# Four tiles of the first product by seven products of quarters, and the casts of v on ScalarE

## The chip, the cores and the metric

The kernel runs on one core of one Trainium2 chip, in one launch. The metric is the device time of that launch in microseconds (us). The time before is the median of three runs.

## The reference, cut to what matters

```python
B, H, S, D = 4, 8, 768, 64                      # attention with a decaying state
gamma = 1.0 - 2.0 ** (-5.0 - np.arange(H))
for t in range(S):
    state = gamma * state + outer(k[t], v[t])   # per batch and head, 64 x 64
    y[t] = (1 / sqrt(D)) * q[t] @ state
x = y.transpose(0, 2, 1, 3).reshape(3072, 512)  # tokens x d_model
h = x @ w_in                                    # first product, d_ff = 2048
g = max(h, 0) + alpha * min(h, 0)
out = g @ w_out                                 # second product, 3072 x 512, f32
```

## The kernel before

**Units and blocks.** The tokens are cut into 12 units of 256 (`U`); three units make a batch. Two units make a block of 512 tokens (`TB`), and there are six blocks, 0 to 5 (`NBLK`). The attention of a unit gives its part of `xT`, the transposed input of the first product. All matmuls take f16 and sum in f32 in the eight PSUM banks; the number given to `ps` is the bank, and a new tile in a bank waits until the last reader of the old one is done.

**First product (`ffn1`).** It has 16 tiles of 128 rows of d_ff (`NFT`). A tile is four matmuls, 512 wide, into one bank. Then ScalarE computes `hm = relu(-h)`, and VectorE makes the gate: `gt = hm * (1 - alpha) + h`, in f16. The tile buffers `hm` are three. In blocks 2 to 5 the tiles are made in pairs, 0, 8, 1, 9 and so on to 7, 15 (`HF` is 8).

**Second product (`ffn2_seven`).** In blocks 1 to 5 it is made by seven products of quarters (Strassen's scheme in Winograd's form) instead of eight: the gates are cut in two by d_ff (`k`) and in two by unit, `w_out` likewise. The sums of quarters of `w_out` are made once (`w_sums`, tile `wsum`), those of the gates in each block (`g_sums`, tile `gs`, numbers 0 to 3). Each product is 16 matmuls, 256 wide. The first product reads gate tiles 0 to 7 of the first unit in that order, the second one tiles 8 to 15, the third one `gs` number 1.

**Order.** The scheduling is manual: each engine runs its instructions in the order in which they are issued, and an instruction that waits holds back all behind it on its engine. `ffn1` and `ffn2_seven` are generators, one `yield` for each matmul; `tick(gen, m)` issues m of them. In a block n of the loop at the end, `ffn1(n)` comes first, and between its matmuls GpSimd rescales k and q of the next block's two units (`rescale`, L152) and casts their v (`cast_v`, L168); SP issues the transposes (`turn_dma`) and loads k, q and v of the units after (`load`). Then `ffn2_seven(n)` is issued, and in its gaps the next block's attention: state sums (`sum_mm`, banks 2 and 3), scores (`score_mm`, banks 4 and 5, then 6 and 7), masks on VectorE (`masks`, L280), state updates on VectorE and GpSimd (`state_sum`, L240, L241), and the outputs (`out_mm`), which ScalarE copies to `xT` (`take_y`, L331). VectorE's `g_sums` numbers 0 and 1 are issued after gate tiles (for f below 4 after tile 11, the rest after tile 15), numbers 2 and 3 between the masks. `behind` makes a GpSimd rescale wait for a VectorE sum.

**Copies of results.** In `ffn2_seven`, `kept` copies a bank to an SBUF tile `cu` (ScalarE, L480), and `plus` adds a bank and such a tile into a tile `os` (VectorE, L485), which SP stores.

Of the kernel before, what the change touches and what calls it, by code (L numbers as in the profile page):

```python
# [9 lines left out]
FP = mybir.dt.float32  # L10
F16 = mybir.dt.float16
COPY = mybir.ActivationFunctionType.Copy
SUB = mybir.AluOpType.subtract
RELU = mybir.ActivationFunctionType.Relu
MULT = mybir.AluOpType.mult
# [6 lines left out]
def kernel(  # L22
# [59 lines left out]
    HF, HM = NFT // 2, d_model // 2  # L82
    wsum = sbp.tile([128, 4, HF, HM], F16, tag="wsum", name="wsum")

    def ps(bank, name, dt=FP, n=512):
        return psp.tile([128, n], dt, tag=f"b{bank}", name=name)

# [52 lines left out]
    def unit(u):  # L140
        if u not in prepped:
            prepped[u] = (
                sbp.tile([128, 2, 2, H, D], F16, tag="kdq", bufs=4, name=f"kdq{u}"),
                sbp.tile([128, 4 * NP, 128], F16, tag="kq", bufs=4, name=f"kq{u}"),
                sbp.tile([128, H, 2, D], F16, tag="vx", bufs=4, name=f"vx{u}"),
            )
        return prepped[u]

# [127 lines left out]

    def masks(u, hh, parts=(0, 1)):
        for a in parts:
            m2 = sbp.tile([128, 2, 2, 128], F16, tag=f"m2{a}{hh}", bufs=2, name=f"m2{a}{hh}")
            i = nc.vector.tensor_tensor(  # L280
                out=m2,
                in0=live[u, hh][a].rearrange("p (r a i) -> p r a i", r=2, a=2),
                in1=mask.unsqueeze(2).to_broadcast([128, 2, 2, 128]),
                op=MULT,
            )
            live[u, hh][a] = m2
        return i
# [37 lines left out]
    def take_y(u, cs):  # L325
        n, ul = divmod(u, 2)
        if n not in xT:
            xT[n] = sbp.tile([128, 2, NP, U], F16, tag="xT", bufs=2, name=f"xT{n}")
        ys = live[u]
        for c in cs:  # L330
            nc.scalar.activation(  # L331
                out=xT[n][:, ul, :, 128 * c : 128 * c + 128].rearrange(
                    "k a (p r) -> k a r p", r=2
                ),
                in_=ys[c].rearrange("k (a r p) -> k a r p", r=2, p=64),
                func=COPY,
                bias=0.0,
                scale=1.0,
            )
# [21 lines left out]
        )[i]  # L361
        return nc.vector.tensor_tensor(out=o, in0=a, in1=b, op=op)  # L362

    def ffn1(n, banks, apart=0):


        gt = sbp.tile([128, NFT, TB], F16, tag="gt", bufs=2, name=f"gt{n}")
        gts[n] = gt
        turns = [(f, 2, ul, ul + 1) for ul in range(2) for f in range(0, apart, 2)]
        rest = range(apart, NFT)  # L370
        if apart == 0:
            rest = [f + x for f in range(HF) for x in (0, HF)]
        turns += [(f, 1, 0, 2) for f in rest]
        for i, (f0, nf, lo, hi) in enumerate(turns):
            hps = ps(banks[i % len(banks)], "hps").rearrange("p (f t) -> p f t", f=nf)
            for f in range(nf):
                for hp in range(4):
                    nc.tensor.matmul(  # L378
                        out=hps[:, f, :].rearrange("p (u t) -> p u t", t=U),
                        lhsT=w_in_all[:, hp, 128 * (f0 + f) : 128 * (f0 + f) + 128],  # L380
                        rhs=xT[n][:, lo:hi, hp, :],
                        start=(hp == 0),
                        stop=(hp == 3),
                    )
                    if f < nf - 1 or hp < 3:
                        yield
            hm = sbp.tile([128, TB], FP, tag="hm", bufs=3, name="hm")
            hm = hm.rearrange("p (f t) -> p f t", f=nf)
            nc.scalar.activation(out=hm, in_=hps, func=RELU, bias=0.0, scale=-1.0)  # L389
            for f in range(nf):  # L390
                nc.vector.scalar_tensor_tensor(  # L391
                    out=gt[:, f0 + f, U * lo : U * hi],
                    in0=hm[:, f, :],
                    scalar=oma_sb[:, f0 + f : f0 + f + 1],
                    in1=hps[:, f, :],
                    op0=MULT,
                    op1=ADD,
                )
            if n > 0 and f0 in ((HF + 3, NFT - 1) if apart == 0 else (NFT - 1,)):

                lo = 0 if apart or f0 < NFT - 1 else 4
                hi = HF if f0 == NFT - 1 else 4
                g_sums(n, 0, lo, hi)
                g_sums(n, 1, lo, hi)
            yield

    def ffn2(n, banks, parts=1):
        gt = gts.pop(n)
        opss = {}
        step = NFT // parts  # L410
        for f0 in range(0, NFT, step):
            for tq in range(4):
                if f0 == 0:
                    opss[tq] = ps(banks[tq % len(banks)], "ops")
                for ft in range(f0, f0 + step):
                    nc.tensor.matmul(  # L416
                        out=opss[tq],
                        lhsT=gt[:, ft, 128 * tq : 128 * tq + 128],
                        rhs=w_out_all[:, ft, :],
                        start=(ft == 0),  # L420
                        stop=(ft == NFT - 1),
                    )
                    if ft == NFT - 1:
                        tag = ("os", "cu")[tq % 2]
                        os_sb = sbp.tile([128, d_model], FP, tag=tag, bufs=3, name=tag)
                        nc.scalar.activation(
                            out=os_sb, in_=opss[tq], func=COPY, bias=0.0, scale=1.0
                        )
                        row = TB * n + 128 * tq
                        nc.sync.dma_start(out=out[row : row + 128, :], in_=os_sb)  # L430
                    yield

    def ffn2_seven(n, x, y, z=None):
# [41 lines left out]
                        yield  # L475

        def kept(o):
            t = sbp.tile([128, 2, HM], FP, tag="cu", bufs=3, name="cu")
            for to, i in [(t, o[0])] if o[0] is not None else zip((t[:, 0, :], t[:, 1, :]), o[1]):
                nc.scalar.activation(out=to, in_=i, func=COPY, bias=0.0, scale=1.0)  # L480
            return t

        def plus(o, t, name="os"):
            so = sbp.tile([128, 2, HM], FP, tag=name, bufs=3, name=name)
            nc.vector.tensor_tensor(out=so, in0=o[0], in1=t, op=ADD)  # L485
            return so

# [52 lines left out]
    def tick(gen, m=10**6):  # L540
        for _ in range(m):
            if next(gen, 1) == 1:
                return
# [124 lines left out]
    tick(gen, 9)  # L668
    out_mm(2, (4, 5))
    tick(gen, 10)  # L670
    tick(half, 24)
    turn_pe(3, 0, 6)
    tick(half, 8)
    turn_pe(3, 1, 7)
    tick(gen, 9)
    score_mm(3, 0, (4, 5))
# [26 lines left out]
    for n in range(1, NBLK):  # L703
        more = n + 1 < NBLK
        u0 = 2 * (n + 1)
        if n > 1:
            gen = ffn1(n, (7, 2, 3, 1, 0, 6, 5, 4, 7, 1, 0, 4, 5, 6, 7, 1))
            if more:
                for u in (u0, u0 + 1):
                    i = rescale(G, u, 0, 0, 8)  # L710
                    if u == u0:
                        behind(i, gate)
                    rescale(G, u, 1, 0, 8)
                    turn_dma(u)
                    cast_v(G, u)
                    if u + 2 < NU:
                        load(u + 2)
                    tick(gen, 8)
            tick(gen)
        gen = ffn2_seven(n, 0, 1) if more else ffn2_seven(n, (0, 3), 1, 2)  # L720
        if more:
            tick(gen, 8)
            sum_mm(u0, (2, 3))
            sum_mm(u0 + 1, (2, 3), half=1)
            score_mm(u0, 0, (4, 5))
            score_mm(u0, 1, (6, 7))
            state(u0, 0, G)
            masks(u0, 0)
            s01 = state_sum(u0, 1, G)
            masks(u0, 1, (0,))  # L730
            s10 = state_sum(u0 + 1, 0, G)
            masks(u0, 1, (1,))
            tick(gen, 8)
            state_copy(s01, "aa")
            state_copy(s10)
            tick(gen, 17)
            state(u0 + 1, 1, G)
            g_sums(n, 2, 0, HF)
            tick(gen, 15)
            out_mm(u0, (4, 5))  # L740
            score_mm(u0 + 1, 0, (6, 7))
            score_mm(u0 + 1, 1, (2, 3))
            masks(u0 + 1, 0)
            masks(u0 + 1, 1)
            gate = g_sums(n, 3, 0, HF)
            tick(gen, 32)
            out_mm(u0 + 1, (4, 5))
        else:
            tick(gen, 33)
            g_sums(n, 2, 0, HF)  # L750
            g_sums(n, 3, 0, HF)
        tick(gen)
# [30 lines left out]
```

## Time and profile before

| what | value |
|---|---|
| median of 3 runs | 204.46 us (204.45 to 204.72) |
| the profiled execution | 206.04 us, span 204.3 us |
| instructions in the profile | 5491 |
| TensorE clock granted | full in all 40 slices |
| first product of blocks 2 to 5 (64 matmuls, 512 wide) | 13.8 us each |
| second product with attention, blocks 2 to 4 | 15.9 to 16.0 us each |
| gate (L391), 512 wide | 745 ns mean, x84 |
| relu (L389), 512 wide | 597 ns mean, x96 |
| rescale on GpSimd (L152), 1024 wide | 1902 ns mean, x16 |
| cast of v on GpSimd (L168), 1024 wide | 1037 ns mean, x11 |

In the lines of the profile PE is TensorE's matmuls and PEld its weight loads, DVE is VectorE, ACT is ScalarE, POOL is GpSimd and SP is the queue that issues DMAs. A line of the timeline has the start in us from the span's start, the busy time in us, the engine, the line of the kernel, the operation, output and inputs, shape and number of instructions; in brackets is the idle time before it and what ended it. Shown durations reach from the first element to the end of the write, so consecutive instructions overlap a little: what an instruction costs its engine is the distance from start to start.

### The profile page before, as it was taken

What the parts mean: (1) busy time and instruction counts of PE and PEld (TensorE: products, weight loads), DVE (VectorE), ACT (ScalarE), POOL (GpSimd) and SP (SyncE); (2) the same over time, 40 slices, a digit from 0 to 9 for tenths busy, and PEclk for the clock granted to TensorE, in tenths of its full rate; (3) what the DMA queues carried; (4) which work ended last, traced back from release to release, by engine and by line L of the source; (5) the groups of instructions that cost most, each with busy time, mean ns of one, the idle gap of its engine ahead of it and who ended that gap; (6) DMA issues with size and microseconds to landing.
All of it is one profiled execution on the core that took longest, in us unless ns stands there. A gap on an engine that the chain in (4) does not pass through costs nothing.

```text
span 204.3 us, 5491 instructions
## 1 busy us (share of the span) xinstructions
PE 195.2 (96%) x2314; PEld 128.2 (63%) x2314; DVE 157.0 (77%) x246; ACT 101.9 (50%) x169; POOL 83.3 (41%) x96
## 2 busy tenths in 40 slices
PE   7789997999999999999999999999999999999993
PEld 2457543566574788744788644788544888545882
DVE  7794985646899999189998289996489995589841
ACT  2465665236376333477353466333476254466311
POOL 2289117480269553970065960165930250000000
PEclk9999999999999999999999999999999999999999
DMA  5998999599997799399911499910570011200004
GB/s 158 337 234 134 185 253 235 157 249 173 299 346 223 153 340 304 110 258 304 284 46 41 149 250 281 300 55 22 176 166 0 3 52 57 103 0 0 21 33 154
DMA packets 64696, 33.94 MB, mean 166 GB/s; under 512 B 18064, under 2 KB 64160, under 8 KB 64672
## 3 DMA queue, kind: packets, MB, share of 16 engines
q1 hardware_dynamic: 60272, 29.37, 50.0%
q0 software_dynamic: 4224, 4.19, 13.4%
q8 instruction: 18, 0.29, 0.6%
q10 hardware_dynamic: 176, 0.03, 0.1%
q14 instruction: 6, 0.05, 0.1%
HBM read 27.30 MB, written 6.29 MB: 164 GB/s over the span
## 4 chain that ended last, share of the span: by engine, by line
PE 73%; DMA 16%; DVE 3%; POOL 2%; SPq 2%; issue 2%; ACT 0%; POOLq 0%; DVEq 0%
PE hps L378 32%; PE ox L464 16%; PE oy L464 11%; DMA qs<-in_q_dram 6%; PE ops L416 5%; DMA wout<-in_moe_w_out_dram 4%; DMA win<-in_moe_w_in_dram 4%; DMA ks<-in_k_dram 3%; PE y L313 2%; SPq L132 2%; PE sca L268 2%; PE y L298 1%; POOL tf L241 1%; PE st L215 1%; PE oz L464 1%
## 5 line engine op out<-in xcount | busy, mean ns | idle before, releaser
L378 PE MATMUL hps<-xT,win 128*128 128x512 f16 (+1 forms) x432 | 84.5, 355 | 0.1
L391 DVE SCALAR_TENSOR_TENSOR gt<-hm,oma,hps 128x512 f16<-128x512 f32 (+1 forms) x108 | 70.8, 685 | 13.6 <-ACT hm L389 8.1
L389 ACT ACTIVATE hm<-hps 128x512 f32<-128x512 f32 x96 | 57.3, 597 | 33.6 <-PE hps L378 31.4
L378 PEld LDWEIGHTS <-win 128*128 128x128 f16 x432 | 42.0, 98 | 40.3 <-DMA win<-in_moe_w_in_dram 0.8
L464 PEld LDWEIGHTS <-gs 128*128 128x128 f16 x320 | 31.0, 98 | 3.9
L241 POOL TENSOR_TENSOR tf<-ss,tab 128x256 f32<-128x256 f32 x16 | 12.2, 765 | 35.7 <-DVE ss L240 34.7
L464 PEld LDWEIGHTS <-gt 128*128 128x128 f16 x240 | 22.8, 98 | 4.8
L152 POOL TENSOR_TENSOR kdq<-ks,tab 128x1024 f16<-128x1024 f32 (+1 forms) x10 | 17.3, 1729 | 18.8 <-issue 9.8
L480 ACT ACTIVATE cu<-ox 128x512 f32<-128x512 f32 (+1 forms) x18 | 9.5, 526 | 29.9 <-PE ox L464 29.7
L256 POOL CAST tg<-tf 64x256 f16<-64x256 f32 x29 | 14.2, 488 | 20.0 <-DVE tf L237 18.6
L485 DVE TENSOR_TENSOR os<-oy,cu 128x512 f32<-128x512 f32 x14 | 9.6, 689 | 16.2 <-PE oy L464 13.7
L152 POOL TENSOR_TENSOR kdq<-qs,tab 128x1024 f16<-128x1024 f32 (+1 forms) x13 | 20.7, 1594 | 1.9 <-DMA qs<-in_q_dram 1.9
L280 DVE TENSOR_TENSOR m<-sca,mi 128x512 f16<-128x512 f32 x24 | 16.4, 684 | 4.2 <-PE scb L268 4.2
L464 PE MATMUL ox<-wsum,gs 128*128 128x256 f16 x160 | 19.1, 273 | 0.0
L331 ACT ACTIVATE xT<-y 128x512 f16<-128x512 f32 x24 | 16.2, 741 | 5.6 <-PE y L313 5.5
L280 DVE TENSOR_TENSOR m<-scb,mi 128x512 f16<-128x512 f32 x24 | 16.3, 681 | 0.0
L416 PE MATMUL ops<-wout,gt 128*128 128x512 f16 x64 | 15.2, 380 | 0.2 <-DMA wout<-in_moe_w_out_dram 0.2
L168 POOL CAST vx<-vs 128x1024 f16<-128x1024 f32 (+1 forms) x13 | 12.5, 973 | 5.6 <-DMA vs<-in_v_dram 5.6
L362 DVE TENSOR_TENSOR gs<-gt 128x1024 f16<-128x1024 f16 (+1 forms) x14 | 12.9, 922 | 0.3
L254 ACT ACTIVATE tg<-tf 64x256 f16<-64x256 f32 x11 | 4.6, 414 | 15.6 <-POOL tf L241 10.4
L188 ACT ACTIVATE kq<-trb 128x1024 f16<-128x1024 f16 x8 | 8.2, 1024 | 6.7 <-PE trb L182 6.5
L464 PE MATMUL ox<-wout,gt 128*128 128x256 f16 x80 | 10.4, 274 | 0.0
(50 smaller groups left out, 175.1 us busy)
## 6 DMA issues: line engine op xcount, KB each, us to landing
out_dram<-os SPq DMA_DIRECT2D x21, 256.0 KB, 2.3
vs<-in_v_dram SPq DMA_DIRECT2D x10, 512.0 KB, 6.4
ks<-in_k_dram SPq DMA_DIRECT2D x8, 512.0 KB, 4.6
qs<-in_q_dram SPq DMA_DIRECT2D x8, 512.0 KB, 5.5
ks<-in_k_dram SPq DMA_DIRECT2D x8, 256.0 KB, 4.7
qs<-in_q_dram SPq DMA_DIRECT2D x8, 256.0 KB, 4.8
win<-in_moe_w_in_dram POOLq DMA_DIRECT2D x4, 512.0 KB, 8.0
wout<-in_moe_w_out_dram POOLq DMA_DIRECT2D x4, 512.0 KB, 8.5
```

Source lines behind the costliest of these rows:

```text
L152: return eng.tensor_tensor(out=kdq[:, t, :, h0:h1, :].rearrange("p r h d -> p h r d"), in0=staged[u]["kq"[t]][:, h0:h1, :].rearrange("p h ...
L168: eng.tensor_copy(out=o, in_=i)
L241: eng.tensor_tensor(out=t, in0=ss, in1=dec, op=MULT)
L256: nc.gpsimd.tensor_copy(out=o, in_=i)
L280: i = nc.vector.tensor_tensor(out=m2, in0=live[u, hh][a].rearrange("p (r a i) -> p r a i", r=2, a=2), in1=mask.unsqueeze(2).to_broadcast([ ...
L331: nc.scalar.activation(out=xT[n][:, ul, :, 128 * c : 128 * c + 128].rearrange("k a (p r) -> k a r p", r=2), in_=ys[c].rearrange("k (a r p) ...
L362: return nc.vector.tensor_tensor(out=o, in0=a, in1=b, op=op)
L378: nc.tensor.matmul(out=hps[:, f, :].rearrange("p (u t) -> p u t", t=U), lhsT=w_in_all[:, hp, 128 * (f0 + f) : 128 * (f0 + f) + 128], rhs=x ...
L389: nc.scalar.activation(out=hm, in_=hps, func=RELU, bias=0.0, scale=-1.0)
L391: nc.vector.scalar_tensor_tensor(out=gt[:, f0 + f, U * lo : U * hi], in0=hm[:, f, :], scalar=oma_sb[:, f0 + f : f0 + f + 1], in1=hps[:, f, :],
L416: nc.tensor.matmul(out=opss[tq], lhsT=gt[:, ft, 128 * tq : 128 * tq + 128], rhs=w_out_all[:, ft, :], start=(ft == 0), stop=(ft == NFT - 1),)
L464: nc.tensor.matmul(out=o[1][m], lhsT=lhs(f, m), rhs=rhs(f), start=(first and f == 0 and (m == 0 or o[0] is None)), stop=(f == HF - 1), ski ...
```

## The change

In blocks 2 to 5 `ffn1_mixed` takes the place of `ffn1`. Twelve tiles stay as they were. Tiles 0, 1, 8 and 9 (`SEV` is 2 in each half) are made by seven products of quarters: `w_in` is cut by d_model (`k`) and by d_ff, `xT` by d_model and by unit. Each product p1 to p7 is four matmuls, 256 wide. Bank 4 takes p1, and on top of it p6, p7 and p4; bank 5 takes p2, then p5 and on top of it p3. ScalarE keeps bank 4 after p1, p6 and p7 (`kept`), VectorE adds it to bank 5 after p2, p7 and p3 (`plus`), which gives three of the four result quarters in SBUF. For these, ScalarE makes the relu from SBUF and GpSimd makes the gate by two operations (`gate_pool`: a multiplication and an addition). The fourth, after p4, is gated by VectorE from bank 4 in two halves.

The sums of quarters of `w_in` (`wi_sums`, four operations, 512 wide) are made once, on VectorE between the first gates of block 1. The sums of `xT` (`x_sums`, four operations, 512 wide) are made on VectorE for each of blocks 2 to 5, right after the block's `xT` is complete. The first q rescale of a block on GpSimd waits for them (`xgate`).

The sums of gates (`g_sums` 0 and 1) come in three pieces, for tiles 2 to 4 after tile 12, for 5 to 7 and then 0 and 1 after tile 15. The casts of v for units 8 to 11 move from GpSimd, in the first product, to ScalarE, in the second product of the block before. Buffers: `kdq`, `kq` and `vx` go from 4 to 3, masks and `xT` from 2 to 1, `hm` from 3 to 5, `cu` from 3 to 4.

```diff
-                sbp.tile([128, 2, 2, H, D], F16, tag="kdq", bufs=4, name=f"kdq{u}"),
+                sbp.tile([128, 2, 2, H, D], F16, tag="kdq", bufs=3, name=f"kdq{u}"),
...
+    def x_sums(n):
+        t = sbp.tile([128, 4, 2, U], F16, tag="xsum", name=f"xsum{n}")
+        xsum[n] = t
+        (b11, b21), (b12, b22) = (
+            [xT[n][:, j, 2 * k : 2 * k + 2, :] for k in range(2)] for j in range(2)
+        )
+        t1, t2, t3, t4 = (t[:, y] for y in range(4))
+        for o, a, b in ((t1, b12, b11), (t2, b22, t1), (t3, b22, b12), (t4, b21, t2)):
+            i = nc.vector.tensor_tensor(out=o, in0=a, in1=b, op=SUB)
+        return i
...
+        def relu(i):
+            hm = sbp.tile([128, TB], FP, tag="hm", bufs=5, name="hm")
+            nc.scalar.activation(out=hm, in_=i, func=RELU, bias=0.0, scale=-1.0)
+            return hm
...
+        def gate_pool(i, f, j):
+            hm = relu(i).rearrange("p (f t) -> p f t", f=2)
+            nc.gpsimd.tensor_tensor(
+                out=hm, in0=hm,
+                in1=oma_sb[:, f : f + 2].unsqueeze(2).to_broadcast([128, 2, U]),
+                op=MULT,
+            )
+            nc.gpsimd.tensor_tensor(
+                out=gt[:, f : f + 2, U * j : U * j + U],
+                in0=hm, in1=i.rearrange("p (f t) -> p f t", f=2), op=ADD,
+            )
...
+        order = (
+            "n2:7 n10:2 p1a n3:3 p2a n11:6 g11a p6a n4:1 p5a n12:0 s2:5 p7a n5:7 n13:2 g22a"
+            " p4a n6:3 p3a n14:6 g12a n7:1 n15:7 s5:8 s0:2"
+        )
+        banks = {"a": (4, 5)}
...
-            gen = ffn1(n, (7, 2, 3, 1, 0, 6, 5, 4, 7, 1, 0, 4, 5, 6, 7, 1))
+            gen = ffn1_mixed(n)
...
-                    rescale(G, u, 1, 0, 8)
+                    i = rescale(G, u, 1, 0, 8)
+                    if u == u0:
+                        behind(i, xgate)
                     turn_dma(u)
-                    cast_v(G, u)
+                    if n == 2:
+                        cast_v(G, u)
...
             state_copy(s10)
+            if n > 1 and u0 + 2 < NU:
+                cast_v(A, u0 + 2)
             tick(gen, 17)
...
             out_mm(u0, (4, 5))
+            if n > 1 and u0 + 3 < NU:
+                cast_v(A, u0 + 3)
             score_mm(u0 + 1, 0, (6, 7))
...
             out_mm(u0 + 1, (4, 5))
+            xgate = x_sums(n + 1)
```

In `order`, `n7:1` is tile 7 made whole in bank 1, with its relu and gate; `p6a` is product 6, with the copy or the sum that follows it; `g12a` is the relu and GpSimd's gate of the quarter that the sum after p3 completes (`g11a` after p2, `g22a` after p7); `s2:5` is `g_sums` 0 and 1 for tiles 2 to 4 and 10 to 12.

## The prediction

> **What bounds the kernel now.** I read the page's busy shares first, then the stretches of one steady block, then the timelines of TensorE and VectorE at the seam where the second product begins, because the change reshuffles the first product and the seam is where its results are asked for.
>
> ```profile
> PE 195.2 (96%) x2314; PEld 128.2 (63%) x2314; DVE 157.0 (77%) x246; ACT 101.9 (50%) x169; POOL 83.3 (41%) x96
> ```
>
> ```profile
> core 0: us, PE busy (x) PEld busy (x) DVE busy (x) ACT busy (x) POOL busy (x), PEclk, DMA share, GB/s
> ...
> 114.96:128.77 13.81, 13.81 (x67) 6.25 (x64) 11.93 (x18) 8.96 (x15) 5.80 (x5) 1.00 0.97 252
> 128.77:144.68 15.91, 15.91 (x301) 13.95 (x300) 12.20 (x20) 5.68 (x9) 8.55 (x11) 1.00 0.37 115
> ```
>
> The first stretch is ffn1 of block 3, the second is its ffn2 with the attention of the next block. TensorE is busy in all of both, at full clock: the block has no stall to give back, so a gain can only be TensorE work removed, and any new wait of TensorE is paid in full. VectorE is at 11.93 of 13.81 in ffn1.
>
> ```profile
> 114.96 13.98 PE L378 MATMUL hps<-xT,win 128*128 128x512 f16 x64
> 128.77 1.07 PE L464 MATMUL ox<-wout,gt 128*128 128x256 f16 x8
> ...
> 131.73 1.91 PE L464 MATMUL oy<-wout,gt 128*128 128x256 f16 x16
> 133.48 1.91 PE L464 MATMUL ox<-wsum,gs 128*128 128x256 f16 x16
> ```
>
> ```profile
> 124.81 5.54 DVE L391 SCALAR_TENSOR_TENSOR gt<-hm,oma,hps 128x512 f16<-128x512 f32 x8
> 130.38 0.69 DVE L362 TENSOR_TENSOR gs<-gt 128x1024 f16<-128x1024 f16 x1
> 131.11 0.69 DVE L362 TENSOR_TENSOR gs<-gs,gt 128x1024 f16<-128x1024 f16 x1
> 131.72 0.41 DVE L240 TENSOR_TENSOR ss<-tf,st 128x256 f32<-128x256 f32 x1
> ```
>
> ```profile
> 128.10 2.25 DVE L391 SCALAR_TENSOR_TENSOR gt<-hm,oma,hps 128x512 f16<-128x512 f32 x3
> ```
>
> One 512-wide matmul is 13.81 / 64 = 0.2158 us from start to start, a 256-wide one 1.75 / 16 = 0.1094. Gates (L391) follow each other at (128.10 - 124.81) / 5 = 0.658 and take 0.745. The last three gates start at 128.10, 128.76 and 129.60. Tile 7 is the last but one, so its gate ends at 129.50. The first product of ffn2 reads tiles 0 to 7 in order and wants tile 7 at 128.77 + 7 x 0.1094 = 129.54. The slack is 0.04 us: whatever makes the gate of tile 7 later stops TensorE.
>
> **The change, part by part.** *TensorE.* Four tiles of four 512-wide matmuls (16 x 0.2158 = 3.45) become seven products of four 256-wide ones (28 x 0.1094 = 3.06): 0.39 us less in each of four blocks, 1.56 in all. That price holds for weights that change at every matmul, as in the rows of L464.
>
> *VectorE in ffn1.* Out go four gates (4 x 0.658 = 2.63). In come three sums of PSUM and SBUF (like L485, 0.60 from start to start: 134.78 to 135.38), two half gates (by-form rows give 745 ns for 512 wide and 476 for 256, so 0.658 - 0.27 = 0.39 each), and the sums of gates in three pieces instead of two. Total 2.58 plus about 0.3: VectorE gets 0.25 more work in a stage that is 0.39 shorter. How long a piece of sums takes: 2048 wide 1.14, 1024 wide 0.61, so 768 is about 0.475 and 512 0.345, plus 0.12 for one that needs the one before (131.11 - 130.38 = 0.73).
>
> *The queue, from the stage's first matmul as zero.* A tile takes 0.863 on TensorE and a quarter product 0.4375, so the order ends tiles and products at: 2 at 0.86, 10 at 1.73, p1 2.16, 3 at 3.03, p2 3.46, 11 at 4.33, p6 4.77, 4 at 5.63, p5 6.07, 12 at 6.93, p7 7.37, 5 at 8.23, 13 at 9.09, p4 9.53, 6 at 10.39, p3 10.83, 14 at 11.69, 7 at 12.56, 15 at 13.42. ScalarE's relu starts 0.20 after a tile (115.82 to 116.02 in the trace), takes 0.60, and the gate starts 0.03 later (116.65). Until tile 12 VectorE still waits for TensorE; the gate of 12 starts at 6.93 + 0.83 = 7.76. From there VectorE is never idle: gate 12 to 8.42, two sums (tiles 2 to 4) to 9.48, sum of p7 to 10.08, gates 5 and 13 to 11.40, two half gates of p4 to 12.18, gate 6 to 12.84, sum of p3 to 13.44, gate 14 to 14.10. The sum of p3 gives its result at 12.84 + 0.69 = 13.53, and ScalarE's relu of it (g12a) stands ahead of the relu of tile 7. ScalarE is in order, so the relu of 7 starts at about 14.04 (two relus follow each other at 0.5), ends at 14.63, and gate 7 runs from 14.66 to 15.41.
>
> TensorE ends ffn1 at 13.42 and wants tile 7 at 13.42 + 0.77 = 14.19. It waits 1.22 plus 0.06 for the signal (in block 1 a mask ends at 76.02 and its matmul starts at 76.08): 1.28 us where 0.39 was saved. Four blocks: 4 x (1.28 - 0.39) = 3.56 us slower.
>
> *What that wait covers.* Tile 15 takes bank 7, which the second head group's scores want 1.75 after ffn1; its gate ends at 16.06, or 2.65 after, and with TensorE 1.28 late the wait is over. The sums of tiles 0 and 1 end at about 17.9, or 4.5 after; the third product asks 4.7 + 1.28 after (last block: 3.5 + 1.28). The last mask comes 8.1 after, and its matmul asks at 7.27 + 1.28. So no second wait is added, by 0.3 us in the tightest place.
>
> *GpSimd.* Six operations of 512 f32 per block. L241 takes 0.61 for 256, L152 1.03 to 1.10 for 512 and 1.90 for 1024, all with one broadcast operand; an add with two full operands is not in the trace. Bounds are 0.61 and 1.90; I take 1.05, the row of the same width. The gate of p7 then ends on GpSimd at 10.86 + 2.1 = 12.96, ahead of relu 7, which needs its buffer hm (fifth of five). The Trainium skill (GPSIMD Engine Reference, Performance versus the Vector engine) gives 4497 ns for a two-input add of 2048 fp32; an estimate from it for 512 is 1.1 to 1.2 us, and the sum would be the same.
>
> *GpSimd beside VectorE.* In block 2 GpSimd still casts v, so after the x sums (ended about -0.4) it runs q, v, k, q, v until 7.26 and the first gate pair until 9.36, beside VectorE's sums from 8.42. Two-SBUF-input sums beside GpSimd: the 1024-wide wsum took 1.10 at 55.79 beside GpSimd against 0.68 alone. So +0.42 in that block, which moves all gates behind. The Trainium skill (SBUF — State Buffer, Practical consequences) says that a VectorE operation with two SBUF inputs and a GpSimd operation that reads SBUF exclude each other for the whole instruction; by that the sums would start at 9.36, 0.94 late, and the time would be 0.5 more.
>
> *At nothing.* The x sums (four of 512 wide, some 1.5 us) fall into VectorE's idle 3.07 before 144.88; without that cover they cost up to 1.5 a block. The q rescale waits for them, from 142.45 to about 144.3; behind it are GpSimd's other rescales and, on SP, the transpose and the loads of the next units. SP issued that transpose at 116.35, 1.4 into ffn1, behind a store, and the rescale now ends at 1.6; the second is level, as no cast stands between. ScalarE's casts (1.0 each, by the 1024-wide L188) fall into its idle 2.7 before the cu at 140.49. Sums of w_in (about 1.5) fall into VectorE's waits of 0.53 and 1.52 ahead of 48.81 and 51.20; uncovered they cost 1.5 once. Fewer buffers: each goes back to a tile whose last reader stands earlier on TensorE.
>
> Sum: 3.56 + 0.42 = 3.98. The profiled span of 204.3 becomes 208.3 (its execution took 206.04, 1.58 above the median of 204.46, a difference I carry over as not belonging to the kernel); the median becomes 208.4.
>
> **Rivals.** *The gates keep up* (faster): all of 1.56 stays, 202.9. For it: VectorE has 1.9 us idle in the old stage and the hm buffers go from three to five. Against: its idle time lies at the front, the slack at tile 7 is 0.04, and gate 7 would have to end 0.9 earlier than I find to break even. *VectorE's queue alone* (slower, less): if relu 7 is not held behind g12a, gate 7 ends at 14.84 and the wait is 0.71: 4 x 0.32 = 1.3, 205.7. If the 768-wide sums cost no more than 512-wide ones, 0.27 comes off each block, about 204.7. *GpSimd decides* (slower, more): from 1.6 us an operation its gate of p7 ends after 14.04 and holds hm against relu 7; at 1.90 that is 14.66, gate 7 ends 0.63 later, and the last sums come after GpSimd's third pair at 18.5, so that masks wait 0.35 in two blocks and the last block's third product 0.5: about 212. *The products save nothing*: if a 256-wide matmul took 0.123 instead of 0.1094, 28 would cost the old 16; but L378's own 256-wide matmuls in block 1 ran at 2.63 / 24 = 0.1096.
>
> **How the numbers follow.** The forecast has 0.55, VectorE's queue alone 0.2, GpSimd 0.13, gates that keep up 0.07, products that save nothing 0.05 (it adds 1.56 to the forecast). 0.2% (0.4 us) is about what a measurement of this kernel can tell from no change. Faster 0.07; within it 0.04, the low end of the second case; slower 0.89. The range reaches from close to that low end, 204.9, to 210.9: the forecast with the rule's 0.5 and half of GpSimd's 3.7.
>
> **What the changed profile would show.** Right: TensorE idle about 1.3 us some 0.77 into ffn2, released by a gate; 28 quarter matmuls in about 3.06; relu 7 after g12a; the bank 7 and mask waits absent. Wrong: TensorE without idle at that seam, the wait in another place (a bank, GpSimd, a DMA), or quarter products slower than 0.44.

## The result and the profile after

The median is 212.62 us (four runs, 211.60 to 213.15) against 204.59 for the kernel before (204.45 to 206.52). The ratio is 1.0364, interval 1.0288 to 1.0440: slower by 8.0 us. The forecast was 4.0 us slower: the direction and the main mechanism were right, and the measured time lies above its range. The profiled execution of the changed kernel took 212.18 us, with a span of 210.5.

The page's busy shares of the changed kernel:

```profile
span 210.5 us, 5678 instructions
PE 194.6 (92%) x2362; PEld 133.1 (63%) x2362; DVE 167.4 (80%) x278; ACT 109.1 (52%) x185; POOL 107.7 (51%) x116
```

TensorE has 0.6 us less work than before (195.2) and 6.2 us more span, so all of the loss is idle time of TensorE. VectorE has 10.4 us more work.

**A stretch that compares exactly.** The time ahead of block 2 differs between executions of one and the same kernel: block 2 starts at 84.99 in the profile of before and at 84.17 in another of that kernel (experiment 1). From there on the two agree to 0.01 us. So I compare the *stretch*: from the start of block 2's first matmul to the start of the last matmul of all. Before, it is 84.99 to 200.60, 115.61 us. After, it is 83.99 to 206.73, 122.74 us. The change costs 7.13 us there. This also squares the two profiled executions: 206.04 + 7.13, less the 1.00 by which block 2 started earlier, is 212.17, and 212.18 was measured.

Block 3 of the changed kernel in the stretches view (columns as in the prediction: time, busy time and instructions of each engine, clock, DMA), first `ffn1_mixed`, then the second product with the attention:

```profile
116.95:130.38 13.43, 13.43 (x78) 7.43 (x76) 10.53 (x17) 8.85 (x16) 9.82 (x7) 1.00 0.95 248
130.38:147.96 17.58, 16.16 (x302) 14.01 (x301) 15.76 (x27) 8.52 (x13) 8.91 (x13) 1.00 0.36 112
```

The first product takes 13.43 (13.81 before): the promised saving of 0.38 is there, and TensorE is busy in all of it at full clock. The second stage takes 17.58 (15.91 before) and TensorE is busy for only 16.16 of it. VectorE's work moved with it: 11.93 + 12.20 became 10.53 + 15.76, so 2.15 us more in a block: 1.40 less beside the first product and 3.56 more behind it.

Where TensorE stands still, in the timeline of the same block (start, busy time, engine, line, operation, in brackets the idle time and what ended it; L470 is a quarter product, L409 whole tiles, L629 the second product):

```profile
127.36 0.60 PE L470 MATMUL hy<-xT,visum 128*128 128x256 f16 x4
127.79 2.75 PE L409 MATMUL hps<-xT,win 128*128 128x512 f16 x12
130.38 0.93 PE L629 MATMUL ox<-wout,gt 128*128 128x256 f16 x7
132.72 0.28 PE L629 MATMUL ox<-wout,gt 128*128 128x256 f16 x1 [1.42 <-DVE gt L429]
```

Seven matmuls of the first product run, and the eighth, which reads gate tile 7, waits for a gate (L429). It was due at 130.38 + 7 x 0.1094 = 131.15 and ran at 132.72; from the start of the product to the next matmuls on TensorE it is 2.56 us where it was 1.00. That is 1.56 us in each of the four blocks. (The bracket counts from the shown end of the matmul before, so it reads 1.42.)

VectorE and ScalarE in the same block, up to gate 7:

```profile
123.89 1.63 DVE L429 SCALAR_TENSOR_TENSOR gt<-hm,oma,hps 128x512 f16<-128x512 f32 x2 [1.03 <-ACT hm L422]
125.55 0.56 DVE L366 TENSOR_TENSOR gs<-gt 128x768 f16<-128x768 f16 x1
126.14 0.56 DVE L366 TENSOR_TENSOR gs<-gs,gt 128x768 f16<-128x768 f16 x1
126.62 0.68 DVE L488 TENSOR_TENSOR os<-hy,cu 128x512 f32<-128x512 f32 x1
...
129.34 0.74 DVE L429 SCALAR_TENSOR_TENSOR gt<-hm,oma,hps 128x512 f16<-128x512 f32 x1
130.00 0.68 DVE L488 TENSOR_TENSOR os<-hy,cu 128x512 f32<-128x512 f32 x1
130.59 0.74 DVE L429 SCALAR_TENSOR_TENSOR gt<-hm,oma,hps 128x512 f16<-128x512 f32 x1
131.92 1.41 DVE L429 SCALAR_TENSOR_TENSOR gt<-hm,oma,hps 128x512 f16<-128x512 f32 x2 [0.58 <-ACT hm L422]
133.36 0.93 DVE L366 TENSOR_TENSOR gs<-gt 128x768 f16<-128x768 f16 x1
```

```profile
130.77 0.63 ACT L422 ACTIVATE hm<-os 128x512 f32<-128x512 f32 x1 [1.28 <-DVE os L488]
131.31 1.06 ACT L422 ACTIVATE hm<-hps 128x512 f32<-128x512 f32 x2
```

From gate 12 (the second of the first row, at 124.71) to gate 14 VectorE has no idle time. The sum of p3 at 130.00 gives its result to ScalarE's g12a relu at 130.77; behind it stands the relu of tile 7, 131.31, and VectorE, idle for 0.58, starts gate 7 at 131.92. This is the prediction's chain, step by step, only later.

The waits of TensorE over the whole profile (who waits <- for whom: us in all, how often, the longest), the rows that matter here:

```profile
PE ox L629 <- DVE gt L429: 5.7, 4, 1.4
PE hy L470 <- DVE os L488: 1.0, 1, 1.0
PE y L317 <- DVE m L284: 0.6, 2, 0.4
PE scb L272 <- DVE ss L244: 0.3, 1, 0.3
```

The last two, masks and scores, are small here: 0.4 of the masks' 0.6 lies ahead of block 2 (at 75.08), and what is left of both falls into block 2. The second row is block 2: product p3 waits there for the `plus` of p7, because it writes on bank 5. Its cause is two rows, of VectorE and of GpSimd:

```profile
92.59 1.67 DVE L366 TENSOR_TENSOR gs<-gt 128x768 f16<-128x768 f16 x1
94.30 0.56 DVE L366 TENSOR_TENSOR gs<-gs,gt 128x768 f16<-128x768 f16 x1
```

```profile
92.58 1.27 POOL L447 TENSOR_TENSOR gt<-hm,os 128x512 f16<-128x512 f32 x1
```

The first sum of gates takes 1.67 beside GpSimd's addition and 0.56 in block 3, where that addition ended at 125.36, before the sum. It ends only 0.41 after GpSimd's operation (92.58 + 1.27 = 93.85), so about three quarters of its own 0.56 lie behind that.

The 7.13 us by block, as lengths from first product to first product:

| block | before | after | difference | saved | wait at tile 7 | p3 | masks, scores, last products |
|---|---|---|---|---|---|---|---|
| 2 | 29.96 | 32.96 | +3.00 | -0.39 | +1.56 | +1.12 | +0.7 |
| 3 | 29.73 | 31.01 | +1.28 | -0.38 | +1.56 | | +0.1 |
| 4 | 29.95 | 31.36 | +1.41 | -0.38 | +1.56 | | +0.2 |
| 5 (to the last matmul) | 25.97 | 27.41 | +1.44 | -0.38 | +1.56 | | +0.3 |

The last column is what the others leave.

GpSimd's third gate of a block meets VectorE's sums in the same way, and in all four blocks. In block 3 (VectorE's row, the sum at 133.36, stands above):

```profile
132.60 1.27 POOL L447 TENSOR_TENSOR gt<-hm,os 128x512 f16<-128x512 f32 x1
```

The sum takes 0.93 instead of 0.56 and ends 0.42 after GpSimd's operation; in blocks 2, 4 and 5 it takes 0.93, 0.92 and 0.92.

### The profile page after: what moved, and what is told of

The parts are those of the page before. It is cut to its first block, busy times and chain, and to the rows that moved or that the text cites. A ratio compares the mean times of both kernels' runs of the same rounds, so it can differ in the third digit from the quotient of the medians.

```text
span 210.5 us, 5678 instructions
## 1 busy us (share of the span) xinstructions
PE 194.6 (92%) x2362; PEld 133.1 (63%) x2362; DVE 167.4 (80%) x278; ACT 109.1 (52%) x185; POOL 107.7 (51%) x116
## 4 chain that ended last, share of the span: by engine, by line
PE 57%; DVE 17%; DMA 13%; issue 4%; ACT 3%; POOL 2%; SPq 0%; ACTq 0%; DVEq 0%; POOLq 0%
PE ox L629 14%; PE oy L629 10%; PE hps L409 10%; DVE gt L429 8%; DMA qs<-in_q_dram 5%; PE hps L546 5%; PE ops L581 5%; DMA wout<-in_moe_w_out_dram 4%; DMA win<-in_moe_w_in_dram 4%; DVE gs L366 3%; DVE os L488 2%; ACT hm L422 2%; PE y L317 2%; PE kps L95 2%; PE hy L470 2%
## 5 line engine op out<-in xcount | busy, mean ns | idle before, releaser
L409 PE MATMUL hps<-xT,win 128*128 128x512 f16 x192 | 46.7, 379 | 0.0
L429 DVE SCALAR_TENSOR_TENSOR gt<-hm,oma,hps 128x512 f16<-128x512 f32 x48 | 35.1, 745 | 12.9 <-ACT hm L422 11.9
L422 ACT ACTIVATE hm<-hps 128x512 f32<-128x512 f32 x48 | 27.6, 594 | 15.4 <-PE hps L409 15.4
L629 PEld LDWEIGHTS <-gs 128*128 128x128 f16 x320 | 30.9, 98 | 4.3 <-DVE gs L366 0.4
L559 DVE SCALAR_TENSOR_TENSOR gt<-hm,oma,hps 128x256 f16<-128x256 f32 (+1 forms) x44 | 25.1, 599 | 6.3 <-ACT hm L557 4.4
L629 PEld LDWEIGHTS <-gt 128*128 128x128 f16 x240 | 22.7, 98 | 11.1 <-DVE gt L429 6.8
L409 PEld LDWEIGHTS <-win 128*128 128x128 f16 x192 | 18.8, 98 | 15.8
L546 PE MATMUL hps<-xT,win 128*128 128x256 f16 (+1 forms) x176 | 28.4, 321 | 0.0
L441 POOL TENSOR_TENSOR hm<-hm,oma 128x512 f32<-128x512 f32 x12 | 12.5, 1041 | 28.8 <-ACT hm L422 28.8
L557 ACT ACTIVATE hm<-hps 128x512 f32<-128x512 f32 x32 | 19.1, 597 | 9.3 <-PE hps L546 9.3
L156 POOL TENSOR_TENSOR kdq<-qs,tab 128x1024 f16<-128x1024 f32 (+1 forms) x13 | 21.2, 1634 | 5.2 <-DVE xsum L393 4.5
L546 PEld LDWEIGHTS <-win 128*128 128x128 f16 x176 | 17.1, 98 | 10.6
L284 DVE TENSOR_TENSOR m<-sca,mi 128x512 f16<-128x512 f32 x24 | 16.4, 685 | 3.7 <-PE scb L272 3.7
L629 PE MATMUL ox<-wsum,gs 128*128 128x256 f16 x160 | 19.1, 273 | 0.1
L284 DVE TENSOR_TENSOR m<-scb,mi 128x512 f16<-128x512 f32 x24 | 16.4, 681 | 0.0
L366 DVE TENSOR_TENSOR gs<-gt 128x768 f16<-128x768 f16 (+2 forms) x18 | 16.0, 890 | 0.3
L629 PE MATMUL ox<-wout,gt 128*128 128x256 f16 x80 | 10.9, 274 | 5.7 <-DVE gt L429 5.7
```

Of the source, the lines that this page charges most:

```text
L156: return eng.tensor_tensor(out=kdq[:, t, :, h0:h1, :].rearrange("p r h d -> p h r d"), in0=staged[u]["kq"[t]][:, h0:h1, :].rearrange("p h ...
L284: i = nc.vector.tensor_tensor(out=m2, in0=live[u, hh][a].rearrange("p (r a i) -> p r a i", r=2, a=2), in1=mask.unsqueeze(2).to_broadcast([ ...
L409: nc.tensor.matmul(out=hps.rearrange("p (u t) -> p u t", t=U), lhsT=w_in_all[:, hp, 128 * f : 128 * f + 128], rhs=xT[n][:, :, hp, :], star ...
L422: nc.scalar.activation(out=hm, in_=i, func=RELU, bias=0.0, scale=-1.0)
L429: nc.vector.scalar_tensor_tensor(out=gt[:, f, U * lo : U * hi], in0=hm[:, c], scalar=oma_sb[:, f : f + 1], in1=i[:, c], op0=MULT, op1=ADD,)
L546: nc.tensor.matmul(out=hps[:, f, :].rearrange("p (u t) -> p u t", t=U), lhsT=w_in_all[:, hp, 128 * (f0 + f) : 128 * (f0 + f) + 128], rhs=x ...
```

## The experiments

**Theory.** VectorE is the bound: from tile 12 to the end of the next masks its queue has no room, so every us of work that the change puts there stops TensorE somewhere, at tile 7 first. **Rivals.** One item alone is late (the relu of tile 7 behind g12a) and another order cures it; or ScalarE's hold, GpSimd's gates, or the change's other edits (sums of `xT` and `w_in`, buffers, casts) cost the time.

**1. The kernel before, again.**

> The kernel before, once more, for a second profile. Theory: blocks 2 to 5 repeat to 0.1 us (first product 13.8, second 15.9), and what differs between executions lies ahead of block 2 (its first product started at 85.0 in the first profile). Rival: the blocks themselves vary by 0.5 us or more.

Median 205.14 (204.31 to 206.07), ratio 0.9996 (0.9964 to 1.0028). The stretch is 115.60 us against 115.61, with block 2 starting at 84.17 instead of 84.99. What varies between executions lies ahead of block 2, and differences of 0.1 us in the stretch can be read from one profile, as long as the granted clock is full in it. It is in every profile compared here but that of experiment 6.

**2. Everything but the seven products.** Blocks 2 to 5 make 16 whole tiles in the old order; the sums of `w_in` and `xT`, the casts, the buffers and `xgate` stay.

```diff
-            gen = ffn1_mixed(n)
+            gen = ffn1_whole(n, (7, 2, 3, 1, 0, 6, 5, 4, 7, 1, 0, 4, 5, 6, 7, 1))
```

> The changed kernel with all 16 tiles made whole again in blocks 2 to 5, in the order of before; the sums of w_in and xT are still made (and not used), the casts, gates on the rescale and buffer counts stay. Theory (the loss lies in the seven products' gates and nothing else): as before within 0.4 us. Rival (the added sums, the x gate or the fewer buffers cost time ahead of block 2): about 1 us above before, with block 2 starting later.

Median 205.16, ratio 0.9997 (0.9964 to 1.0029), and a stretch of 115.61: the kernel before, to 0.01 us. So the other edits are covered, as the prediction said, and all 7.13 us come with the seven products. This kernel's code ahead of block 2 is that of the changed kernel, and it loses nothing there either.

**3. Block 2's casts of v off GpSimd.** ScalarE casts v of units 6 and 7 too, in block 1's second product, so that GpSimd's first gate is done before VectorE's first sum.

```diff
-                    if n == 2:
-                        cast_v(G, u)
...
-            if n > 1 and u0 + 2 < NU:
+            if u0 + 2 < NU:
                 cast_v(A, u0 + 2)
```

(and the same for `u0 + 3`)

> The changed kernel, with the casts of v for units 6 and 7 moved to ScalarE too, so that GpSimd is free earlier in block 2. Theory (VectorE's sums of gates wait for the whole GpSimd operation beside them): block 2's sums take 0.6 instead of 1.67, its length falls from 33.0 to about 31.3, the time by 1.6 us. Rival (block 2 is long for another reason, loads or the x sums): less than 0.3 us.

VectorE's first sum in block 2:

```profile
95.90 0.56 DVE L366 TENSOR_TENSOR gs<-gt 128x768 f16<-128x768 f16 x1
```

It takes 0.56 instead of 1.67, p3's wait is gone, the first product of block 2 takes 13.42 instead of 14.54, and the block 31.83 instead of 32.96. The price of GpSimd beside the sum is thereby shown: 1.12 us (I had expected a block of 31.3). The stretch is 121.57, 1.17 less. The time is worse all the same, 214.07 (213.76 to 214.34, ratio 1.0411, 1.0337 to 1.0484), for a reason that I did not expect, ahead of block 2:

```profile
80.55 1.06 ACT L170 ACTIVATE vx<-vs 128x1024 f16<-128x1024 f32 x1 [2.79 <-DMA vs<-in_v_dram]
```

```profile
82.14 2.58 PE L629 MATMUL ox<-wsum,gt 128*128 128x256 f16 x16 [2.17 <-ACT cu L645]
```

The load of that v had not landed. ScalarE waits 2.79 us for it, the copy of a bank (`cu`) is queued behind, and TensorE waits 2.17 for the copy. In this execution the granted clock was also half from 83.2 to 86.6, right behind the wait, and the last 32 matmuls of block 1 took 5.16 instead of 32 x 0.1094 = 3.5. The three other executions, at a mean clock of 0.997 to 0.999, took 213.76 to 214.24, so the kernel is late without that as well.

**4. The relu of tile 7 ahead of g12a.** The rival of one late item: g12a goes behind tiles 7 and 15.

```diff
-            " p4a n6:3 p3a n14:6 g12a n7:1 n15:7 s5:8 s0:2"
+            " p4a n6:3 p3a n14:6 n7:1 n15:7 g12a s5:8 s0:2"
```

> The changed kernel, with the relu and gate of the third quarter (g12a) put behind tile 15, so that ScalarE's relu of tile 7 is not held behind it. Theory (ScalarE's order adds to VectorE's queue): gate 7 starts 0.6 us earlier, TensorE's wait for it falls from 1.58 to about 1.0 in each of blocks 2 to 5, 2.4 us in all. Rival (VectorE's queue alone sets it): the wait stays, under 0.4 us in all; and if GpSimd decides, the last sums come later and masks wait, so that it is slower.

The wait at tile 7 falls from 1.56 to 0.88 in each block, so ScalarE's hold is real. The stretch falls by only 0.16, where I had expected 2.4, to 122.58 (median 211.65, ratio 1.0298, 1.0233 to 1.0363). TensorE's waits show where the rest went:

```profile
PE ox L629 <- DVE gt L429: 2.9, 4, 0.7
PE y L317 <- DVE m L284: 1.9, 3, 0.8
PE ox L629 <- DVE gs L366: 0.8, 1, 0.8
```

The masks (L284; 0.4 of their 1.9 lies ahead of block 2) and, in block 5, the product that reads the sums now wait. VectorE's queue did not get shorter. The two sums behind gate 7 took 0.93 and 0.56 in the changed kernel; here they lie beside more of GpSimd's last gate and take 0.63 and 1.51.

```profile
133.49 1.51 DVE L366 TENSOR_TENSOR gs<-gs,gt 128x768 f16<-128x768 f16 x1
```

```profile
133.12 1.46 POOL L447 TENSOR_TENSOR gt<-hm,os 128x512 f16<-128x512 f32 x1
```

**5. The lower half of d_ff first.** Tiles 2 to 7 are made before 10 to 15, so that every gate that the first product reads is early, and the sums come late.

```diff
-            "n2:7 n10:2 p1a n3:3 p2a n11:6 g11a p6a n4:1 p5a n12:0 s2:5 p7a n5:7 n13:2 g22a"
-            " p4a n6:3 p3a n14:6 g12a n7:1 n15:7 s5:8 s0:2"
+            "n2:7 n3:2 p1a n4:3 p2a n5:6 g11a p6a n6:1 p5a n7:0 p7a n10:7 n11:2 g22a"
+            " p4a n12:3 p3a n13:6 s2:5 g12a n14:7 n15:1 s5:8 s0:2"
```

> The changed kernel with tiles 2 to 7 made ahead of tiles 10 to 15, and the last two tiles in banks 7 and 1, so that the second product no longer asks for a tile whose gate is late. Theory (VectorE's queue of ffn1, which ends 18.6 us after the stage's start, is the bound, and TensorE waits for it somewhere): the wait at tile 7 is gone, and comes back at the masks in blocks 2 to 4 and at the third product in block 5; from block 2's first matmul to the last one the 122.7 us fall by 1 to 2. Rival (the wait at tile 7 is the whole loss): by 6.

The wait at tile 7 is gone entirely (0.97 from the first product to the next matmuls). The stretch is 121.97, 0.77 less than after, where I had expected 1 to 2; median 210.87, ratio 1.0283 (1.0247 to 1.0319).

```profile
PE scb L272 <- DVE gt L429: 2.6, 3, 0.9
PE y L317 <- DVE m L284: 1.8, 3, 0.8
PE oy L628 <- DVE gt L429: 1.5, 1, 1.5
```

The scores wait for the bank of tile 14, then the masks are late (0.4 of their 1.8 again lies ahead of block 2), and in block 5 the second product waits for its gates. Block 2's wait at p3 is gone too (its first product takes 13.42). That is 6.24 + 1.12 = 7.4 us less at these two places, and 6.6 of it came back at other places. This is the theory against the rival of one late item: the wait moves with the order and hardly shrinks. Counted from block 3's first matmul, the last of VectorE's sums of gates 0 and 1 ends at 18.72 in the changed kernel, 18.69 in experiment 4 and 18.78 here, and the block takes 31.01, 30.97 and 31.06: the block's length goes with the end of VectorE's queue, whichever place waits.

**6. Less work on VectorE, more on ScalarE.** The factor (1 - alpha) goes into the relu, as a scale for each row; the gate is then one addition (about 0.6 from start to start instead of 0.66), and GpSimd's gate one operation instead of two.

```diff
-            nc.scalar.activation(out=hm, in_=i, func=RELU, bias=0.0, scale=-1.0)
+                nc.scalar.activation(
+                    out=hm[:, c], in_=i[:, c], func=RELU, bias=0.0, scale=neg_sb[:, f : f + 1]
+                )
...
-                nc.vector.scalar_tensor_tensor(
...
+                nc.vector.tensor_tensor(out=gt[:, f, :], in0=i, in1=hm, op=ADD)
```

> The changed kernel with its order, but in blocks 2 to 5 ScalarE's relu takes -(1 - alpha) as its scale for each row, so that a gate is one addition: VectorE's costs 0.60 instead of 0.66 and the half gates of p4 one 0.60 instead of 0.78, GpSimd's pair of operations becomes one (1.3 instead of 2.3), and ScalarE makes the quarters' relus in two halves. Theory (VectorE's queue, and GpSimd beside its sums): the wait at tile 7 falls by some 0.25 a block only, as the relu of 7 is still held; block 2's first sums no longer wait 1.1; in all 2 to 3 us less than the 122.7. Rival (TensorE's own work or the order of products): no change.

A miss: I had expected 2 to 3 us less, and got 215.24, ratio 1.0499 (1.0450 to 1.0547), and a stretch of 124.75, 2.0 longer than after. Most of these 2.0 us are not the edit's. In block 3 the granted clock was half for 3.4 us (133.5 to 136.9), and sixteen matmuls, 256 wide, followed each other at 0.21 instead of 0.11:

```profile
134.56 3.06 PE L629 MATMUL oy<-wout,gt 128*128 128x256 f16 x16
```

An estimate from that: half of 3.4 us is 1.7, so the stretch at full clock would be 123.0, 0.3 longer than after. The four executions have mean clocks of 0.984 to 0.992, the changed kernel's 0.998 to 1.000, so the medians don't compare the two edits either; why the clock fell is open. The blocks at full clock, 2, 4 and 5, take 32.04, 31.75 and 27.76: block 2 is 0.92 shorter, its wait at p3 gone, and the others 0.39 and 0.35 longer. So even at full clock the gain is block 2's alone. Two of ScalarE's costliest groups have the reason (behind the count busy us and mean ns, then the idle time before and what ended it):

```profile
L425 ACT ACTIVATE hm<-hps,neg 128x512 f32<-128x512 f32 x48 | 31.5, 682 | 12.5 <-PE hps L410 11.1
L557 ACT ACTIVATE hm<-hps 128x512 f32<-128x512 f32 x32 | 19.1, 597 | 9.4 <-PE hps L546 9.3
```

In one kernel, the relu with a scale for each row takes 682 ns and the one with a constant 597; two in a row stand 0.57 apart instead of 0.48, and the quarters need two of 256 each, so that g12a holds back the relu of 7 for 0.82 instead of 0.54. That lies ahead of gate 7, whose wait grows from 1.56 to 2.13 us in each block. The queue theory as I had it, VectorE alone, is too narrow: ScalarE's path into gate 7 counts as well.

**7 and 8. Both, and both with the casts.** Experiments 5 and 6 together; then that with the casts of v 6 and 7 on ScalarE ahead of block 2's matmuls.

> Both of these edits together. Theory: VectorE's queue ends about 4.0 after TensorE instead of 5.2, the masks are in time, and only block 2 and the third product of block 5 wait, 0.5 each; the stretch from block 2's first matmul to the last takes about 115, as before the change or 0.5 less. Rival (ScalarE, with 22 operations in ffn1, becomes the bound): 117 or more.

> As the kernel with both edits, and ScalarE casts v of units 6 and 7 right ahead of block 2's first relu, where it stood idle for 2.0 us, instead of GpSimd between its rescales. Theory (in block 2 the sums wait for GpSimd): block 2 becomes as long as block 4, up to 0.7 less than with both edits. Rival: the two casts hold up the first relus and nothing is gained.

Stretches of 124.14 and 124.15, at full clock, where I had expected about 115 and up to 0.7 less (medians 214.05 and 214.61, ratios 1.0451, 1.0411 to 1.0491, and 1.0466, 1.0431 to 1.0502). That is 2.2 longer than the same order without the scaled relu (experiment 5), so here the edit does cost 2 us. With the low half first the late place is the scores again, and VectorE itself waits for ScalarE at the gate of p4. The slower relus explain that; no run takes them apart from the rest of the edit.

```profile
127.85 0.69 DVE L437 TENSOR_TENSOR gt<-hx,hm 128x512 f16<-128x512 f32 x1 [0.83 <-ACT hm L425]
```

The casts change nothing here, since in this order no sum stands early in block 2.

**9. No sums of gates 0 and 1.** The strongest test of the bound: blocks 2 to 5 leave these sums out, and the two products that read them take plain quarters of the gates. TensorE's work is unchanged; the result is another one.

```diff
-                g_sums(n, 0, int(lo), int(hi))
-                g_sums(n, 1, int(lo), int(hi))
+                pass
...
-        yield from product(ox, gs(1), ws(1), False)
+        yield from product(ox, gs(1) if n < 2 else gq(0, 1), ws(1), False)
```

(and the same for `gs(0)`; sum 3, which reads sum 1, takes a gate quarter in its place)

> The changed kernel without the sums of gates 0 and 1 in blocks 2 to 5 (left out: 3.1 us of VectorE a block; the two products that read them take gate quarters instead, so the result is another). Theory (VectorE's queue is what TensorE waits for): the wait at tile 7 falls from 1.56 to some 0.5, the waits in block 2's first product, at the masks and in block 5 vanish, and the stretch from block 2's first matmul to the last falls from 122.7 to about 116. Rival (ScalarE's and GpSimd's gates of the quarters are the bound): it falls by less than 2.

The stretch is 117.53: 5.2 of the 7.13 us are gone (median 207.09, ratio 1.0139, 1.0101 to 1.0177). The waits on masks, scores and p3 are back at those of before, and one row is left:

```profile
PE ox L628 <- DVE gt L429: 3.1, 4, 0.9
```

So TensorE's waits follow VectorE's queue. The test takes out more than the change put in: VectorE is busy for 23.11 in block 3, 26.28 after and 24.13 before, so 5.2 is no measure of the added work alone. What stays, 0.9 us at tile 7, is the chain through ScalarE: the sum of p3, g12a, the relu of 7, its gate. I had expected 0.5 there.

**10. One more operation in the kernel before.** The slack of 0.04 us at tile 7, tested by itself: an addition of 512 on VectorE after the gate of tile 5, its output read by nothing, and no other change.

```diff
+            if n > 1 and f0 == 5:
+                nc.vector.tensor_tensor(out=spin, in0=hps[:, 0, :], in1=hm[:, 0, :], op=ADD)
```

> The kernel before with one more VectorE operation of 0.60 us (an addition of 512 whose result nobody reads) behind the gate of tile 5 in blocks 2 to 5. Theory (the slack of gate 7 is 0.04 us): TensorE waits 0.6 at tile 7 in each block, and the stretch from block 2's first matmul to the last grows from 115.6 to 118.0. Rival (VectorE's 1.9 us of idle time in the stage absorb it): no change.

In block 3, VectorE's addition and TensorE's wait:

```profile
125.44 0.68 DVE L400 TENSOR_TENSOR spin<-hps,hm 128x512 f16<-128x512 f32 x1
```

```profile
127.42 0.93 PE L466 MATMUL ox<-wout,gt 128*128 128x256 f16 x7
128.81 0.28 PE L466 MATMUL ox<-wout,gt 128*128 128x256 f16 x1 [0.46 <-DVE gt L391]
```

The operation costs VectorE 0.60 from start to start (125.44 to 126.04), and tile 7 comes 0.60 later in each block: 1.60 from the first product to the next matmuls instead of 1.00. The stretch grows by 2.20 (median 207.07, ratio 1.0132, 1.0097 to 1.0167); blocks 3 and 4 grow by the full 0.60, block 2 by 0.42, since another small wait in it shrinks. VectorE's idle time early in the stage absorbs none of it at tile 7.

**11. A smaller dose.** Only tiles 0 and 8 by seven products (`SEV` 1), in blocks 2 to 4, the low half first, block 5 whole. TensorE should save about half, and VectorE's additions are half as wide. The last gates lie in banks 5, 7 and 1.

```diff
-    SEV = 2
+    SEV = 1
...
-            gen = ffn1_mixed(n)
+            gen = ffn1_mixed(n) if more else ffn1_whole(n, ...)
```

> A smaller form: only tiles 0 and 8 by seven products, in blocks 2 to 4, tiles 1 to 7 ahead of 9 to 15, the last gates in banks 5, 7 and 1, block 5 whole. TensorE has 0.2 less a block. Theory: VectorE ends 0.7 later against TensorE than before the change, which the masks (1.2 of slack) take; only block 2, with its casts on GpSimd, waits; the stretch from block 2's first matmul to the last is 115.0 to 115.6. Rival (any added VectorE work comes back as a wait): 116.5 or more.

The stretch is 118.04, 2.43 longer than before, where I had expected 115.0 to 115.6: this is the forecast's rival, any added work of VectorE comes back as a wait (median 207.60, ratio 1.0152, 1.0128 to 1.0176). The first product takes 13.69 in blocks 3 and 4, 0.12 less than whole; the waits at scores and masks take more than that. Of the masks' row, 0.4 lies ahead of block 2:

```profile
PE y L317 <- DVE m L284: 1.3, 3, 0.5
```

No version run here beats the kernel before.

## Why the prediction was right and wrong

**Right.** The bound (TensorE without a gap, 0.04 us of slack at tile 7) and where it breaks. The saving: 0.39 a block forecast, 0.38 to 0.39 measured. The mechanism: gate 12 was due 7.76 after the stage's start and came at 124.71 - 116.95 = 7.76; g12a stood ahead of the relu of 7, and gate 7 stopped the eighth matmul. The covers of the sums of `xT` and `w_in`, the casts and the buffers held (experiment 2). Of the rivals, "VectorE's queue alone" supposed that without ScalarE's hold most of the loss goes; experiment 4 took the hold away and kept the loss.

**Wrong in size: 3.98 forecast, 7.13 measured in the stretch.** The steps that failed are "so no second wait is added" and GpSimd beside VectorE counted for block 2 alone, and there too small. Three terms make nearly all of the 3.15 us, and a fourth lies outside.

1. *The wait at tile 7, 1.28 forecast, 1.56 measured; four times 0.28 is 1.1 us.* The chain lost 0.2 at one place and 0.1 at another. The first sum started 8.60 after the stage's start instead of 8.42: it reads the gate just made and waited until that was written, and I had paid the 0.12 for a dependent operation only between the two sums. All gates behind moved by 0.2 (gate 6 at 12.39, forecast 12.18). Then the way through ScalarE: 0.77 from the start of the sum of p3 to g12a's start (0.69 forecast) and 0.54 from there to the relu of 7 (0.51 forecast).

2. *"So no second wait is added, by 0.3 us in the tightest place": 1.3 us measured, 0.7 of it in block 2.* I had compared the end of VectorE's queue with TensorE's demands place by place, each with TensorE already late, and called a margin of 0.3 enough. The sums of gates 0 and 1 end 5.29 after the first product in block 3, forecast 4.5: 0.3 of this is the later gate 7, 0.1 the same wait for a gate just made, and 0.37 GpSimd's third gate beside the first of these sums. By my own figures that gate ran from about 14.2 (13.53 and a relu) for 2.1, to 16.3, and so over the sums' start at 15.98 (14.66 and two gates), in every block; I put this at nothing. In block 5 the third product waits 0.26 for these sums, so the 0.37 alone is enough to make it late. In block 2, where the scores lost 0.2 in the kernel before already, the masks take 0.4 and the scores 0.3 more; experiment 3 leaves these 0.7, so the casts of v are not their cause, and why block 2 has less room there is open. Experiments 4 and 5 show the general form of the error: behind tile 7 the queue runs at the edge at every later place too. The prediction's sign "mask waits absent" failed with it.

3. *GpSimd beside VectorE in block 2, +0.42 forecast, 1.12 measured at p3.* I took the price of the nearest row (a 1024-wide sum, 1.10 instead of 0.68). But that sum, begun at 55.79, ended 0.55 after GpSimd's operation of 55.42 to 56.34, as this one ended 0.41 after its own: the 0.42 was what was left of that operation, and no price of a sum. Here the sum took 1.67 instead of 0.56, and experiment 3 gave the 1.12 back in full when GpSimd was out of the way. The prediction let that delay move the gates only; it first delayed the sum of p7, which holds bank 5 against p3 on TensorE, a wait of its own inside the first product. The Trainium skill (SBUF — State Buffer, Who interferes with whom, the practical consequences) has the rule that such a sum and a GpSimd operation that reads SBUF exclude each other for the whole instruction; I had set it aside for the row. The trace agrees with it: 1.67 beside GpSimd here, 0.93 behind gate 15 and 1.51 in experiment 4, each ending 0.41 to 0.42 after GpSimd's operation. Gates and sums with one operand in PSUM were not held: in block 3, beside GpSimd's addition of 129.22 to 130.50, gate 6 at 129.34 takes its 0.74 and the sum of p3 at 130.00 its 0.68.

4. *The baseline.* I carried 1.58 us, by which the profiled execution of before exceeded the median, as something that does not belong to the kernel. It was an execution with a longer part ahead of block 2, of a kind that runs of either kernel show. The medians differ by 8.0, the stretches by 7.13. Experiment 2 has the changed kernel's code ahead of block 2 and the median of before, so the remaining 0.9 is most likely chance in that part over four runs; no run here settles it.

**GpSimd's price.** Forecast 1.05 for each operation. Its multiplication with a broadcast operand took 1.04, the addition with two full ones 1.27, so 2.3 a gate instead of 2.1. Its own length did not decide: between its gates GpSimd waits 2.75 us for ScalarE in block 3. The Trainium skill's figure (GPSIMD Engine Reference, Performance versus the Vector engine), estimated down to 1.1 to 1.2, lies between the two.

The sum of the range's upper end, 208.4 + 0.5 + half of 3.7, is 210.8 and not 210.9, which changes nothing here.

**Left open.** Why the granted clock halved in the profiles of experiments 3 and 6, why the relu with a scale for each row is 85 ns slower, and which item makes the 0.2 us of masks and scores in block 4 against 0.1 in block 3.

## What to carry to other kernels

Work taken from a fully busy engine is worth only what the engines behind it can take on: here 0.39 us of matmuls a block were bought with 2.15 us of VectorE work, on a VectorE with 0.04 us of slack at the point of hand-over. Before trading, add one useless operation to the helper engine and see whether the time moves (experiment 10: 0.60 in, 0.60 out). When a reordering takes a wait away, look for the same microseconds at the next places that read the same queue before believing the gain, and compare kernels over a stretch that repeats exactly rather than by medians alone, after a look at the granted clock in it.

## What the runs showed of the hardware

- A VectorE sum of two f16 SBUF operands beside a GpSimd addition on SBUF operands: 1.67, 1.51 and 0.93 instead of 0.56 us for 768 wide, ending 0.41 to 0.42 after that addition, wherever in it the sum began. GpSimd's operation grew in experiment 4, 1.46 instead of 1.27.
- At half the granted clock (3.4 us in experiment 6's profile) 256-wide matmuls followed each other at 0.21 us, at full clock at 0.11.
- ScalarE's relu, 512 wide: 0.60 us from PSUM with a constant scale (0.48 from start to start), 0.63 from SBUF (0.54), 0.68 with a scale for each row (0.57).
- GpSimd, 512 wide from f32: 1.04 us with one broadcast operand, 1.27 with two full ones and f16 output.
- A ScalarE cast put ahead of a copy of a bank passes on the lateness of its DMA: 2.79 us of waiting for v became 2.17 us of TensorE's.
